# A hand-built schedule's activity sum for zero matmuls, and the table of thresholds that goes with it

## Chip, cores and metric

The kernel runs on one core of a Trainium2 chip. The metric is the device time of one execution in microseconds (us); times of the kernel before are the median of three runs. A core has five engines with their own instruction streams: TensorE (PE; its weight loads are listed as PEld), VectorE (DVE), ScalarE (ACT), GpSimd (POOL) and SyncE (SP, which issues the transfers). They meet through semaphores. TensorE's clock is granted by a throttle, and the profile lists the granted share.

## The reference

Four residual layers over 2048 tokens of width 512 with 32 heads of 16. Layers 0 and 2 are `_A_ref`: attention inside four segments of 512 tokens under the reference's mask, gated with a linear memory that is carried from segment to segment. Layers 1 and 3 are `_B_ref`: full attention over 2048 tokens. Cut to what matters:

```python
# A, for each segment s
logits = einsum('bhqd,bhkd->bhqk', qs, ks) * scale + mask
a_dot  = einsum('bhqk,bhkd->bhqd', softmax(logits), vs)
a_mem  = (phi(qs) @ M) / (phi(qs) @ z + 1e-6)
o      = g * a_mem + (1 - g) * a_dot
M, z   = M + phi(ks).T @ vs, z + phi(ks).sum()
# B
o = einsum('bhqk,bhkd->bhqd', softmax(q @ k.T * Dh ** -0.5), v)
# all
x = x + A(layernorm(x)); x = x + B(layernorm(x))   # twice, with the same weights
```

## The kernel before

The kernel is a Python program that writes out the instruction order of every engine in advance. `Sched.add` appends an instruction to its engine's list, works out what it must wait for, and calls `Sched.estimate`, which keeps a planned clock for each engine. The `Builder` reads these planned clocks whenever it decides what to put next, so one changed decision can shift everything after it.

The work comes in units. A unit takes two or three blocks of 128 keys by 512 queries of one head. TensorE computes the scores of a block with one matmul over 16 of the 32 rows that it addresses (four such row groups run side by side); the scores go into three PSUM banks; ScalarE takes the exponential of all of them in one instruction (line 1514), into `pT`. Units alternate between two sets of three banks, so TensorE fills one set while ScalarE empties the other. Later, TensorE multiplies the exponentials with the values. Where the output is token-major, these are matmuls with 34 or 51 streamed columns; in most of layers 1 and 3 (`fm`), the values are the 17 stationary columns (16 values and a column of ones for the denominator), 512 columns stream, and four such matmuls run side by side in four column groups of the array. They and the row-split score matmuls are what the weights of the activity sum distinguish, with tile shapes `rows < 128` and `cols < 128`.

ScalarE has more exponentials than it has time, so some blocks go to VectorE. `dx_first` (line 1121) writes a block's scores as 16-bit integers whose bits, read as bf16, approximate an exponential; `dx_shift` (line 1184) adds constants for further chords of the approximation, for one, two or four blocks at once. The tables call these decisions `DX_...`, `TAKEN`, `REST`, `QREST` and `PAIRS2`. Projections, layer norms, memory updates and output projections are background tasks, fitted between units by `background`, `bg_one` and `fits`, under credits `CR_...` and margins.

`keep_busy` is called at the end of each unit. It issues zero matmuls (a zero 128 by 128 weight against 512 columns of `wB`, which adds nothing to the result) while the activity of the last 3413 ns is below `FILL`, at most `FILLS` in a unit:

```python
        at = max(self.sc.t["act"] - 1330, min(soon, default=0.0) - self.HOR)
        while n < self.FILLS and self.sc.streamed(max(self.sc.t["pe"], at), 3413) < self.FILL:
            self.mm(self.ps[:, bank.col0:bank.col0 + 512], self.zero[:, :], self.wB[:, 0, 0:512], not own, not own,
```

`streamed` sums the weights that `estimate` has put into `self.streams` for each matmul. Before, a matmul counts its streaming time times 0.285 with fewer than 128 rows, times 0.38 with fewer than 128 columns, and in full otherwise.

`PIECES` is a table of 44 entries. When ScalarE's planned clock passes the first number (in us), the entry's values overwrite the builder's thresholds, so each 40 us stretch of the kernel has thresholds of its own.

Of the kernel before, what the change touches and what calls it, by code (L numbers as in the profile page):

```python
# [255 lines left out]


class Builder:
    NPU, NDX, FIT, MARGIN, PART, FILL_DVE, EARLY, FILL = 4, 5, 2, 450, 1, 300, 700, 0.5
# [11 lines left out]
    PIECES = [(20.0, {'DXA_REST': 14, 'EVAC_ACT': -300, 'LOW': 32}),  # L271
              (60.0, {'AHEAD': 500, 'CR_W': 1900, 'DXA_REST': 10, 'EVAC_ACT': -300, 'LOW': 24, 'wide': True}),
              (100.0, {'AHEAD': 500, 'CR_W': 1900, 'DQ': 1900, 'EVAC_ACT': -300, 'wide': True}),
              (140.0, {'AHEAD': 300, 'CR_W': 1400, 'DQ': 2200, 'DX_T': 480, 'EVAC_ACT': 0}),
              (180.0, {'DMA_LATE': 300, 'DX_FIN': 2500, 'DX_T': 480, 'PE_B': 5, 'PE_LOW': 5}),
              (220.0, {'DMA_LATE': 600, 'DX_FIN': 2000, 'DX_T': 430, 'LOW': 16, 'PE_B': 4, 'PE_LOW': 6, 'PVN': 6}),
              (260.0, {'DX_RES': 2, 'HOR': 100, 'LOW': 24, 'NEAR_N': 200, 'PVN': 4}),
              (300.0, {'DX_RES': 2, 'HOR': 100, 'MARGIN': 700, 'NEAR_N': 200}),
              (340.0, {'DMA_LATE': 300, 'DQ': 1900, 'DX_RES': 2, 'FILLS': 1, 'HOR': 100, 'MARGIN': 700, 'NEAR_E': 80, 'NEAR_N': 200}),
              (380.0, {'DMA_LATE': 300, 'DMA_STEPS': 3, 'DQ': 2500, 'DX_RES': 2, 'DX_T': 330, 'FILLS': 1, 'HOR': 100, 'MARGIN': 700, 'NEAR_E': 0, 'NEAR_N': 200}),  # L280
              (420.0, {'DMA_LATE': 300, 'DMA_STEPS': 3, 'DQ': 2500, 'DX_RES': 2, 'DX_T': 330, 'FILLS': 1, 'HOR': 100, 'MARGIN': 700, 'NEAR': 6, 'NEAR_E': 0, 'NEAR_N': 200}),
              (460.0, {'ALTA': (1, 9, 9, 9), 'DMA_LATE': 300, 'DMA_STEPS': 3, 'DQ': 2500, 'DX_RES': 2, 'DX_T': 330, 'FILLS': 1, 'HOR': 100, 'MARGIN': 700, 'NEAR': 10, 'NEAR_E': 0, 'NEAR_N': 200, 'TAKEN': 1.5}),
              (500.0, {'ALTA': (1, 1, 9, 9), 'CR_W': 1250, 'DMA_LATE': 600, 'DMA_STEPS': 2, 'DQ': 2200, 'DQN': 300, 'DX_RES': 0, 'DX_T': 430, 'FILLS': 2, 'HOR': 400, 'MARGIN': 450, 'NEAR_E': 60, 'NEAR_N': 130, 'TAKEN': 2.7}),
              (540.0, {'ALTA': (1, 1, 1, 1), 'CR_W': 1400, 'DQ': 2500, 'DQN': 600, 'PE_A': 4}),
              (580.0, {'DQ': 2200, 'FILLS': 1, 'FILL_DVE': 450, 'PART': 3, 'PE_A': 5}),
              (620.0, {'FILLS': 1, 'FILL_DVE': 450, 'NEAR_S': 30, 'PART': 3, 'SLACK': 150}),
              (660.0, {'FILLS': 2, 'FILL_DVE': 300, 'NEAR_S': 60, 'PART': 1, 'SLACK': 0}),
              (700.0, {'MARGIN': 700, 'SLACK': 0, 'TAKEN': 2.4}),
              (740.0, {'DQ': 2500, 'DX_LATE': 1500, 'MARGIN': 700, 'SLACK': 0, 'TAKEN': 2.4}),
              (780.0, {'DQ': 2200, 'DX_LATE': 3000, 'MARGIN': 450, 'PVHOLE': 250, 'PVLATE': 600, 'SLACK': 300, 'TAKEN': 2.7}),  # L290
              (820.0, {'BG_BANK': 0, 'PVHOLE': 100, 'PVLATE': 900, 'TAKEN': 3}),
              (860.0, {'AHEAD': 200, 'BG_BANK': 200, 'TAKEN': 2.7}),
              (900.0, {'AHEAD': 200, 'DX_LATE': 1500, 'DX_RES': 1}),
              (940.0, {'AHEAD': 200, 'DX_LATE': 1500, 'DX_RES': 1, 'FILL_DVE': 150, 'MARGIN': 700}),
              (980.0, {'AHEAD': 200, 'DX_LATE': 1500, 'DX_RES': 1, 'FILL_DVE': 150, 'MARGIN': 700, 'REST': 14}),
              (1020.0, {'AHEAD': 200, 'DVE_FIN': 1000, 'DX_LATE': 1500, 'DX_RES': 1, 'FILL_DVE': 150, 'MARGIN': 700, 'PART': 3, 'REST': 14}),
# [1 line left out]
              (1100.0, {'CARRY_W': 300, 'DMA_STEPS': 3, 'DXA_REST': 26, 'FILL': 0.35, 'LOW': 4, 'REST_N': 20}),
              (1140.0, {'CARRY_W': 0, 'DMA_STEPS': 2, 'DXA_REST': 10, 'FILL': 0.5, 'FILLS': 3, 'LOW': 4, 'PVN': 3, 'REST_N': 14}),
              (1180.0, {'FILLS': 3, 'LOW': 4, 'NEAR_S': 30, 'PVN': 2}),  # L300
              (1220.0, {'FILLS': 3, 'LOW': 4, 'MARGIN': 700, 'NEAR_S': 30, 'PVN': 2}),
              (1260.0, {'DVE_FIN': 1000, 'FILLS': 3, 'LOW': 4, 'MARGIN': 700, 'NEAR_S': 30, 'PVN': 2}),
              (1300.0, {'AHEAD': 200, 'BG_BANK': 400, 'DVE_FIN': 1000, 'DX_RES': 1, 'FILLS': 3, 'FILL_DVE': 150, 'LOW': 4, 'MARGIN': 700, 'NEAR_S': 30, 'PVN': 2}),
# [1 line left out]
              (1380.0, {'AHEAD': 200, 'BG_BANK': 400, 'DVE_FIN': 1000, 'DX_RES': 1, 'FILL': 0.45, 'FILLS': 3, 'FILL_DVE': 150, 'LOW': 4, 'MARGIN': 700, 'NEAR_S': 30, 'PVN': 2}),
              (1420.0, {'AHEAD': 200, 'BG_BANK': 400, 'DVE_FIN': 1000, 'DX_RES': 1, 'FILL': 0.45, 'FILLS': 3, 'FILL_DVE': 150, 'LOW': 4, 'MARGIN': 700, 'NEAR_S': 30, 'PVN': 2}),
              (1460.0, {'AHEAD': 200, 'BG_BANK': 400, 'DVE_FIN': 1000, 'DX_RES': 1, 'EVAC_ACT': -300, 'FILL': 0.45, 'FILLS': 2, 'FILL_DVE': 150, 'LOW': 4, 'MARGIN': 700, 'NEAR_S': 30, 'PVN': 2, 'REST': 14, 'REST_N': 20}),
              (1500.0, {'AHEAD': 200, 'BG_BANK': 400, 'DVE_FIN': 1000, 'DX_RES': 1, 'EVAC_ACT': -300, 'FILL': 0.45, 'FILL_DVE': 150, 'LOW': 4, 'MARGIN': 700, 'NEAR_S': 30, 'PVN': 2, 'REST': 14, 'REST_N': 20}),
              (1540.0, {'AHEAD': 200, 'BG_BANK': 400, 'DVE_FIN': 1000, 'DX_RES': 1, 'EVAC_ACT': -300, 'FILL': 0.45, 'FILL_DVE': 150, 'LOW': 4, 'MARGIN': 700, 'NEAR_S': 30, 'PVN': 2, 'REST': 11, 'REST_N': 20}),
              (1580.0, {'AHEAD': 200, 'BG_BANK': 400, 'DVE_FIN': 1000, 'DX_RES': 0, 'EVAC_ACT': -300, 'FILL': 0.45, 'FILL_DVE': 150, 'LOW': 4, 'MARGIN': 700, 'NEAR_S': 30, 'PVN': 2, 'REST': 5, 'REST_N': 20, 'TAKEN': 3.5}),  # L310
              (1620.0, {'AHEAD': 200, 'BG_BANK': 400, 'DVE_FIN': 1000, 'EVAC_ACT': -300, 'FILL': 0.45, 'FILL_DVE': 150, 'LOW': 4, 'MARGIN': 700, 'NEAR_S': 30, 'PVN': 2, 'REST': 5, 'REST_N': 20, 'TAKEN': 3.5}),
              (1660.0, {'AHEAD': 300, 'BG_BANK': 200, 'DVE_FIN': 600, 'DX_T': 530, 'EVAC_ACT': 0, 'FILL': 0.5, 'FILL_DVE': 300, 'LOW': 24, 'MARGIN': 450, 'NEAR_N': 200, 'NEAR_S': 60, 'PVN': 4, 'REST': 11, 'REST_N': 14, 'TAKEN': 3, 'TAKEN_N': 4}),
              (1700.0, {'DVE_FIN': 1000, 'DX_T': 530, 'NEAR_N': 200, 'TAKEN': 3, 'TAKEN_N': 4}),
              (1740.0, {'DVE_FIN': 1000, 'DX_T': 530, 'NEAR_N': 200, 'REST': 8, 'TAKEN': 3, 'TAKEN_N': 4})]
# [1571 lines left out]
```

## Time and profile before

| | us |
|---|---|
| median of three runs | 1774.92 |
| lowest, highest | 1773.96, 1778.8 |
| the profiled execution | 1777.42 |
| its span, first to last instruction | 1775.7 |
| mean granted TensorE clock in it | 0.989 |
| zero matmuls, TensorE busy with them | 175, 61.1 |

The page of the profile gives, in this order, the busy time of each engine, a picture of the span in 40 slices, the transfer queues, the chain of work that ended last and the costliest groups of instructions. In a row of a group stand the line, the engine, the operation, output and input, the shapes and the count; then busy time in us and mean ns of one; then the idle time of the engine just before, and what ended it. Matmuls have one line (445), since a helper issues them all, so they are told apart by their tiles. Four matmuls that run side by side show overlapping times; the engine's busy time counts each moment once. In the windows view, each row is a stretch of the span, with the busy time and (in brackets) the instructions of each engine, then the granted clock.

### The profile page before, as it was taken

The numbers are of one execution on the slowest core, as the hardware profiler recorded it, in microseconds if no ns is written. First come the engines' busy times: TensorE is split into PE (matmuls) and PEld (weight loads), VectorE is DVE, ScalarE is ACT, GpSimd is POOL, SyncE is SP. The second block draws the span as 40 slices with busy tenths as digits, with TensorE's granted clock in tenths as the row PEclk, the third lists the DMA queues.
The fourth block names the chain that finished last, engine by engine and source line by source line (L and its number), as shares of the span: only waits on it lengthen the run. The fifth ranks groups of instructions, "written<-read, shape, count | busy, mean of one in ns | idle before, by whom it ended". The sixth has DMA issues, their size and how long they took to land.

```text
span 1775.7 us, 42674 instructions
## 1 busy us (share of the span) xinstructions
PE 1586.7 (89%) x17429; PEld 564.7 (32%) x17429; DVE 1520.6 (86%) x3016; ACT 1733.2 (98%) x1680; POOL 287.4 (16%) x656
## 2 busy tenths in 40 slices
PE   8889899999998999999999989999888888888887
PEld 4445454452223222323222332332222222222222
DVE  6677867499985999798999789767999999999998
ACT  7999999999999999999999999999999999999998
POOL 4622415110005000203000330241100000000000
PEclk9999999999999999999999999999999999999999
DMA  6121111000101000000000010010000000000000
GB/s 173 22 47 32 29 17 26 14 12 4 16 7 16 1 13 13 8 13 19 1 13 13 16 23 13 16 22 13 2 13 1 1 1 13 1 1 7 7 1 13
DMA packets 86180, 30.01 MB, mean 17 GB/s; under 512 B 78816, under 2 KB 85472, under 8 KB 85984
## 3 DMA queue, kind: packets, MB, share of 16 engines
q1 hardware_dynamic: 85984, 27.29, 7.5%
...
q14 instruction: 60, 0.49, 0.1%
...
## 4 chain that ended last, share of the span: by engine, by line
ACT 50%; PE 22%; issue 16%; DVE 9%; POOL 2%; DMA 1%; SPq 0%; ACTq 0%; DVEq 0%; POOLq 0%
ACT pT L1514 49%; PE ps L445 22%; POOL pT L1529 2%; DVE KB L1121 1%; DVE VB L1121 1%; DVE dxw L1184 1%; ACT amem L697 0%; DVE dxw L1121 0%; DVE QA L1121 0%; DMA xT<-xn 0%; DVE KA L1121 0%; DVE KA L1646 0%; DVE KB L1184 0%; DVE x L911 0%; DVE VB L1184 0%
## 5 line engine op out<-in xcount | busy, mean ns | idle before, releaser
L1514 ACT ACTIVATE pT<-ps 128x1024 bf16<-128x1024 f32 (+4 forms) x1627 | 1700.1, 1193 | 27.9 <-PE ps L445 19.8
L445 PE MATMUL ps<-qm,KB 32*128 32x512 bf16 x3584 | 524.0, 386 | 97.8 <-ACT pT L1514 87.0
L445 PE MATMUL ps<-pT,VB 128*17 128x512 bf16 x2217 | 378.9, 387 | 10.5 <-ACT pT L1514 6.0
L1529 POOL TENSOR_SCALAR_AFFINE_SELECT pT<-pT 128x256 bf16<-128x256 bf16 (+2 forms) x524 | 211.8, 416 | 545.0 <-ACT pT L1514 533.0
L445 PEld LDWEIGHTS ps<-qm,KB 32*128 32x128 bf16 x3584 | 132.3, 91 | 465.7 <-ACT pT L1514 360.5
L1424 POOL TENSOR_SCALAR qm<-QB,par 128x512 bf16<-128x512 bf16 x88 | 68.2, 777 | 856.4 <-PE ps L445 782.8
L445 PEld LDWEIGHTS ps<-pT,VB 128*17 128x17 bf16 x2217 | 87.6, 87 | 244.2 <-issue 198.9
L1121 DVE TENSOR_SCALAR dxw<-ps 128x512 uint16<-128x512 f32 (+1 forms) x209 | 143.6, 698 | 5.3 <-PE ps L445 4.4
L445 PE MATMUL ps<-qm,QA 32*128 32x512 bf16 x512 | 111.4, 391 | 25.4 <-ACT pT L1514 22.7
L1184 DVE TENSOR_SCALAR dxw<-dxw 128x1024 uint16<-128x1024 uint16 (+1 forms) x315 | 125.2, 409 | 3.0 <-PE ps L445 1.3
L1121 DVE TENSOR_SCALAR QA<-ps 128x512 uint16<-128x512 f32 (+1 forms) x174 | 122.2, 715 | 5.4 <-PE ps L445 4.8
L445 PE MATMUL ps<-qm,KA 32*128 32x384 bf16 (+3 forms) x1024 | 103.4, 307 | 24.2 <-ACT pT L1514 20.0
L445 PE MATMUL ps<-VA,pT 128*128 128x51 bf16 (+1 forms) x2560 | 109.0, 189 | 14.0 <-POOL pT L1529 6.4
L1121 DVE TENSOR_SCALAR VA<-ps 128x512 uint16<-128x512 f32 (+1 forms) x159 | 114.0, 730 | 6.3 <-PE ps L445 5.5
L445 PE MATMUL ps<-dxw,VW 128*17 128x512 bf16 x435 | 110.6, 383 | 0.2 <-DVE dxw L1184 0.2
L445 PEld LDWEIGHTS ps<-VA,pT 128*128 128x128 bf16 x2560 | 86.2, 97 | 63.2 <-POOL pT L1529 29.7
L1121 DVE TENSOR_SCALAR KB<-ps 128x512 uint16<-128x512 f32 (+1 forms) x128 | 96.2, 769 | 2.8 <-PE ps L445 1.9
L445 PE MATMUL ps<-xT,wA 128*128 128x512 bf16 (+1 forms) x281 | 78.3, 381 | 1.5 <-DVE xT L658 0.9
L445 PE MATMUL ps<-pT,VA 128*17 128x512 bf16 x393 | 78.6, 387 | 1.2 <-ACT pT L1514 0.9
L1121 DVE TENSOR_SCALAR VB<-ps 128x512 uint16<-128x512 f32 (+1 forms) x99 | 74.7, 769 | 3.2 <-PE ps L445 2.6
L445 PE MATMUL ps<-dxw,VB 128*17 128x512 bf16 x256 | 74.3, 381 | 0.0
L445 PE MATMUL ps<-VB,pT 128*128 128x34 bf16 (+1 forms) x1788 | 69.5, 186 | 1.4 <-ACT pT L1514 1.1
...
## 6 DMA issues: line engine op xcount, KB each, us to landing
...
xT<-xn SPq DMA_TRANSPOSE x60, 2.4
oT<-ob SPq DMA_TRANSPOSE x36, 2.4
...
```

What stands on the lines that cost most here:

```text
L445: self.sc.add("pe", lambda e: e.matmul(out, lhsT, rhs, start=start, stop=stop, skip_group_check=True), reads=reads, banks=[(bank, "w", all ...
L1121: self.sc.add("dve", lambda e: e.tensor_scalar(d, o, SCALE * LOG2E * 128, W_C if dxs[0][:3] in self.wt else EXP_C, op0=ALU.mult, op1=ALU.add),
L1184: self.op("dve", lambda e: e.tensor_scalar(o, w, d, None, op0=ALU.add), reads=self.b_dxw[b0][:len(ents)], writes=wr, ns=(295, 425, 560, 69 ...
L1424: self.op(eng, (lambda m, q, col: lambda e: e.tensor_scalar(m, q, col, 0.0, op0=ALU.mult, op1=ALU.add))(m, q, col), reads=[bq, self.b_par] ...
L1514: self.sc.add("act", (lambda dst, src: lambda e: e.activation(dst, src, ACT.Exp, scale=SCALE))(dst, src), writes=self.b_pT[slot * 3 + i:sl ...
L1529: self.op("pool", (lambda blk, pat: lambda e: e.affine_select(blk, blk, pattern=pat, compare_op=ALU.is_ge, fill=0.0, base=0, channel_multi ...
```

## The change

The weights in `estimate` change. Row-split matmuls count 0.3 of their streaming time. Column-split matmuls count 0.85 of the time by which they extend the time already covered by such matmuls (`fm_end` holds its end). Of full matmuls, those with fewer than 100 streamed columns count 0.9. The default of `FILL` goes from 0.5 to 0.44. All 44 entries of `PIECES` are replaced by others with the same boundaries in time; a few are shown.

```diff
-        self.streams = []
+        self.streams, self.fm_end = [], 0.0
...
-            self.streams.append((st, n / 2.4 * (0.285 if rows < 128 else 0.38 if cols < 128 else 1)))
+            if rows < 128:
+                w = 0.3 * n / 2.4
+            elif cols < 128:
+                w = 0.85 * max(0.0, st + n / 2.4 - max(st, self.fm_end))
+                self.fm_end = max(self.fm_end, st + n / 2.4)
+            else:
+                w = n / 2.4 * (0.9 if n < 100 else 1)
+            self.streams.append((st, w))
...
-    NPU, NDX, FIT, MARGIN, PART, FILL_DVE, EARLY, FILL = 4, 5, 2, 450, 1, 300, 700, 0.5
+    NPU, NDX, FIT, MARGIN, PART, FILL_DVE, EARLY, FILL = 4, 5, 2, 450, 1, 300, 700, 0.44
...
-    PIECES = [(20.0, {'DXA_REST': 14, 'EVAC_ACT': -300, 'LOW': 32}),
-              (60.0, {'AHEAD': 500, 'CR_W': 1900, 'DXA_REST': 10, 'EVAC_ACT': -300, 'LOW': 24, 'wide': True}),
...
-              (1060.0, {'AHEAD': 300, 'CARRY_W': 300, 'DVE_FIN': 600, 'DX_LATE': 3000, 'DX_RES': 0, 'FILL': 0.35, 'FILL_DVE': 300, 'MARGIN': 450, 'PART': 1, 'REST': 11, 'REST_N': 20}),
...
-              (1340.0, {'AHEAD': 200, 'BG_BANK': 400, 'DVE_FIN': 1000, 'DX_RES': 1, 'FILL': 0.45, 'FILLS': 3, 'FILL_DVE': 150, 'LOW': 4, 'MARGIN': 700, 'NEAR_S': 30, 'PVN': 2}),
...
+    PIECES = [(20.0, {'CR_A': 1500, 'LOW': 32, 'PE_A': 3, 'TAKEN_N': 2}),
+              (60.0, {'CR_A': 1300, 'FILL': 0.5, 'LOW': 24, 'PE_A': 5, 'TAKEN_N': 3}),
+              (100.0, {'FILL': 0.5, 'FILLS': 1}),
+              (140.0, {'DXS': 2, 'DX_BANK': 300, 'FILL': 0.44, 'FILLS': 2, 'wide': True}),
...
+              (1340.0, {'DX_WAIT': 0, 'PAIRS2': 2, 'PVHOLE': 250, 'QREST': 30}),
...
```

The computation stays the same, with the same matmuls for scores and projections. Which blocks ScalarE takes and which VectorE, which wait for which, and the place of each background task follow from the new table.

More of the change, by code (lines that the diff above doesn't have):

```diff
@@ L270 @@
              [(-1.5, -6.7, -5.8, 20.8, 1.2), (-5.2, -1.6, 28.5, 28, 7), (21, 35.0, 8.2, 30, 27.7), (21, 48.0, 37, 23.6, 12.2)]]
-    PIECES = [(20.0, {'DXA_REST': 14, 'EVAC_ACT': -300, 'LOW': 32}),
-              (60.0, {'AHEAD': 500, 'CR_W': 1900, 'DXA_REST': 10, 'EVAC_ACT': -300, 'LOW': 24, 'wide': True}),
[L273 to L296, printed above, removed]
-              (1060.0, {'AHEAD': 300, 'CARRY_W': 300, 'DVE_FIN': 600, 'DX_LATE': 3000, 'DX_RES': 0, 'FILL': 0.35, 'FILL_DVE': 300, 'MARGIN': 450, 'PART': 1, 'REST': 11, 'REST_N': 20}),
[L298 to L303, printed above, removed]
-              (1340.0, {'AHEAD': 200, 'BG_BANK': 400, 'DVE_FIN': 1000, 'DX_RES': 1, 'FILL': 0.45, 'FILLS': 3, 'FILL_DVE': 150, 'LOW': 4, 'MARGIN': 700, 'NEAR_S': 30, 'PVN': 2}),
[L305 to L314, printed above, removed]
@@ new lines @@
+    PIECES = [(20.0, {'CR_A': 1500, 'LOW': 32, 'PE_A': 3, 'TAKEN_N': 2}),
+              (60.0, {'CR_A': 1300, 'FILL': 0.5, 'LOW': 24, 'PE_A': 5, 'TAKEN_N': 3}),
+              (100.0, {'FILL': 0.5, 'FILLS': 1}),
+              (140.0, {'DXS': 2, 'DX_BANK': 300, 'FILL': 0.44, 'FILLS': 2, 'wide': True}),
+              (180.0, {'CR_A': 1100, 'DXS': 1, 'DX_BANK': 500, 'PART': 4}),
+              (220.0, {'CR_A': 1300, 'MARGIN': 700, 'PART': 1, 'SLACK': 150}),
+              (260.0, {'BG_BANK': 100, 'LOW': 4, 'MARGIN': 700, 'SLACK': 150}),
+              (300.0, {'BG_BANK': 200, 'CR_B': 1700, 'DXS': 0, 'FILL_DVE': 150, 'LOW': 24, 'MARGIN': 700, 'SLACK': 300}),
+              (340.0, {'CR_B': 1500, 'DXS': 1, 'EARLY': 1000, 'FILL_DVE': 300, 'MARGIN': 450}),
+              (380.0, {'DX_RES': 3, 'EARLY': 1000, 'MARGIN': 700}),
+              (420.0, {'DX_RES': 3, 'EARLY': 1000, 'MARGIN': 700, 'PVN': 3}),
+              (460.0, {'DX_RES': 3, 'EARLY': 1000, 'MARGIN': 700, 'PVN': 3}),
+              (500.0, {'DX_RES': 3, 'EARLY': 700, 'MARGIN': 700, 'PVN': 3, 'REST': 8}),
+              (540.0, {'DVE_FIN': 300, 'DX_RES': 3, 'MARGIN': 700, 'PVN': 3, 'REST': 8, 'SLACK': 150}),
+              (580.0, {'DVE_FIN': 300, 'DX_RES': 3, 'DX_T': 480, 'FILL': 0.46, 'MARGIN': 700, 'PVN': 3, 'QREST': 16, 'REST': 8, 'SLACK': 300}),
+              (620.0, {'DVE_FIN': 600, 'DX_RES': 0, 'DX_T': 430, 'FILL': 0.44, 'FILLS': 1, 'MARGIN': 450, 'PVN': 4, 'QREST': 24, 'REST': 11}),
+              (660.0, {'CARRY_W': 300, 'FILLS': 1, 'QREST': 36}),
+              (700.0, {'CARRY_W': 300, 'CR_W': 1250, 'FILLS': 1, 'QREST': 36}),
+              (740.0, {'CARRY_W': 300, 'CR_W': 1250, 'FILLS': 1, 'QREST': 36}),
+              (780.0, {'CARRY_W': 300, 'CR_W': 1250, 'FILLS': 1, 'PVN': 6, 'QREST': 36, 'SLACK': 500}),
+              (820.0, {'CARRY_W': 0, 'CR_W': 1400, 'FILLS': 2, 'FILL_DVE': 150, 'PVN': 4, 'QREST': 24, 'SLACK': 500}),
+              (860.0, {'FILL_DVE': 150, 'NEAR_E': 40, 'PVN': 3, 'REST': 14, 'SLACK': 500}),
+              (900.0, {'AHEAD': 200, 'FILL_DVE': 300, 'NEAR_E': 60, 'PVN': 4, 'REST': 11, 'SLACK': 300}),
+              (940.0, {'AHEAD': 200, 'ALTA': (2, 9, 9, 9), 'FILL_DVE': 450}),
+              (980.0, {'AHEAD': 300, 'ALTA': (1, 1, 1, 1), 'DX_RES': 1, 'FILL_DVE': 300, 'LOW': 12, 'MARGIN': 700}),
+              (1020.0, {'DX_RES': 1, 'FILL_DVE': 450, 'FILL_FREE': 0.5, 'LOW': 12, 'MARGIN': 700}),
+              (1060.0, {'DMA_LATE': 0, 'DX_RES': 1, 'FILL_DVE': 450, 'FILL_FREE': 0.5, 'LOW': 12, 'MARGIN': 700}),
+              (1100.0, {'DMA_LATE': 0, 'DX_RES': 1, 'FILL_DVE': 450, 'FILL_FREE': 0.5, 'LOW': 4, 'MARGIN': 700}),
+              (1140.0, {'CR_LOW': 1300, 'DMA_LATE': 0, 'DX_RES': 1, 'EARLY': 1000, 'FILL_DVE': 450, 'FILL_FREE': 0.5, 'LOW': 4, 'MARGIN': 700, 'NEAR_S': 30}),
+              (1180.0, {'BG_BANK': 400, 'CR_LOW': 1300, 'DMA_LATE': 0, 'DX_RES': 1, 'EARLY': 1000, 'FILL_DVE': 450, 'FILL_FREE': 0.5, 'LOW': 4, 'MARGIN': 700, 'NEAR_S': 30, 'TAKEN_N': 2}),
+              (1220.0, {'BG_BANK': 400, 'CR_B': 1700, 'CR_LOW': 1300, 'DMA_LATE': 0, 'DX_LATE': 1500, 'DX_RES': 1, 'EARLY': 1000, 'FILL_DVE': 450, 'FILL_FREE': 0.5, 'LOW': 4, 'MARGIN': 700, 'NEAR_S': 30, 'REST': 17, 'TAKEN_N': 2}),
+              (1260.0, {'BG_BANK': 400, 'CR_B': 1700, 'CR_LOW': 1300, 'DMA_LATE': 0, 'DX_LATE': 1500, 'DX_RES': 1, 'EARLY': 1000, 'FILL_DVE': 450, 'FILL_FREE': 0.5, 'LOW': 4, 'MARGIN': 700, 'NEAR_S': 30, 'REST': 20, 'SLACK': 500, 'TAKEN_N': 2}),
+              (1300.0, {'BG_BANK': 200, 'CR_B': 1500, 'CR_LOW': 1900, 'DMA_LATE': 600, 'DX_LATE': 3000, 'DX_RES': 0, 'DX_WAIT': 0, 'EARLY': 700, 'FILL_DVE': 300, 'FILL_FREE': 1, 'LOW': 24, 'MARGIN': 450, 'NEAR_S': 60, 'REST': 11, 'SLACK': 300, 'TAKEN_N': 3}),
+              (1340.0, {'DX_WAIT': 0, 'PAIRS2': 2, 'PVHOLE': 250, 'QREST': 30}),
+              (1380.0, {'DX_WAIT': 0, 'PAIRS2': 2, 'PVHOLE': 250, 'QREST': 30}),
+              (1420.0, {'AHEAD': 200, 'DX_WAIT': 0, 'LOW': 4, 'PAIRS2': 2, 'PVHOLE': 250, 'PVN': 6, 'QREST': 30}),
+              (1460.0, {'AHEAD': 200, 'DX_T': 480, 'DX_WAIT': 0, 'FILL_DVE': 700, 'LOW': 4, 'PAIRS2': 2, 'PVHOLE': 250, 'PVN': 6, 'QREST': 30}),
+              (1500.0, {'AHEAD': 200, 'DX_T': 480, 'DX_WAIT': 0, 'FILL_DVE': 700, 'LOW': 4, 'NEAR': 14, 'NEAR_N': 200, 'NEAR_S': 0, 'PAIRS2': 2, 'PVHOLE': 250, 'PVN': 6, 'QREST': 30}),
+              (1540.0, {'AHEAD': 200, 'DVE_LATE': 700, 'DX_T': 480, 'DX_WAIT': 0, 'FILL_DVE': 700, 'LOW': 4, 'NEAR': 14, 'NEAR_N': 200, 'NEAR_S': 0, 'PAIRS2': 2, 'PVHOLE': 250, 'PVN': 6, 'QREST': 30}),
+              (1580.0, {'AHEAD': 300, 'DVE_LATE': 700, 'DX_LATE': 1500, 'DX_T': 480, 'DX_WAIT': 0, 'FILL_DVE': 700, 'GAP': 1, 'LOW': 4, 'NEAR': 14, 'NEAR_N': 200, 'NEAR_S': 0, 'PAIRS2': 2, 'PVHOLE': 250, 'PVN': 6, 'QREST': 30}),
+              (1620.0, {'DVE_LATE': 700, 'DX_LATE': 1500, 'DX_T': 480, 'DX_WAIT': 0, 'FILL_DVE': 700, 'GAP': 1, 'LOW': 4, 'NEAR': 14, 'NEAR_N': 200, 'NEAR_S': 0, 'PAIRS2': 2, 'PVHOLE': 250, 'PVN': 6, 'QREST': 30, 'REST': 14}),
+              (1660.0, {'DVE_LATE': 700, 'DX_LATE': 1500, 'DX_T': 480, 'DX_WAIT': 0, 'EARLY': 1000, 'FILL': 0.46, 'FILL_DVE': 700, 'GAP': 1, 'LOW': 4, 'NEAR': 14, 'NEAR_N': 200, 'NEAR_S': 0, 'PAIRS2': 2, 'PVHOLE': 250, 'PVN': 6, 'QREST': 30, 'REST': 14}),
+              (1700.0, {'DVE_LATE': 700, 'DX_LATE': 1500, 'DX_T': 480, 'DX_WAIT': 0, 'EARLY': 1000, 'FILL': 0.46, 'FILL_DVE': 700, 'GAP': 1, 'LOW': 4, 'NEAR': 14, 'NEAR_N': 200, 'NEAR_S': 0, 'PAIRS2': 2, 'PVHOLE': 250, 'PVN': 6, 'QREST': 30, 'REST': 14}),
+              (1740.0, {'DVE_LATE': 700, 'DX_LATE': 1500, 'DX_T': 480, 'DX_WAIT': 0, 'EARLY': 1000, 'FILL': 0.46, 'FILL_DVE': 700, 'GAP': 1, 'LOW': 4, 'NEAR': 14, 'NEAR_N': 200, 'NEAR_S': 0, 'PAIRS2': 2, 'PVHOLE': 250, 'PVN': 6, 'QREST': 30, 'REST': 5})]
```

## The prediction

> **What bounds the kernel now.** The page comes first: busy time by engine, the chain that ended last, and the costliest group.
>
> ```profile
> span 1775.7 us, 42674 instructions
> ...
> PE 1586.7 (89%) x17429; PEld 564.7 (32%) x17429; DVE 1520.6 (86%) x3016; ACT 1733.2 (98%) x1680; POOL 287.4 (16%) x656
> ...
> ACT 50%; PE 22%; issue 16%; DVE 9%; POOL 2%; DMA 1%; SPq 0%; ACTq 0%; DVEq 0%; POOLq 0%
> ...
> L1514 ACT ACTIVATE pT<-ps 128x1024 bf16<-128x1024 f32 (+4 forms) x1627 | 1700.1, 1193 | 27.9 <-PE ps L445 19.8
> ```
>
> ScalarE is busy 1733.2 of 1775.7 us, 1700.1 of them with the exponentials of line 1514. So the time is ScalarE's work plus the 42.5 us in which it stands. Other engines count only through these 42.5 us, or by taking exponentials off ScalarE. The windows view says where it stands (us, busy time and instructions of PE, PEld, DVE, ACT, POOL, then the granted clock, the DMA share and GB/s):
>
> ```profile
> core 0: us, PE busy (x) PEld busy (x) DVE busy (x) ACT busy (x) POOL busy (x), PEclk, DMA share, GB/s
> 0.00:40.00 40.00, 33.54 (x389) 18.45 (x389) 24.86 (x68) 30.60 (x42) 16.96 (x48) 1.00 0.67 189
> 42.00:47.00 5.00, 5.00 (x51) 2.33 (x51) 1.35 (x4) 4.18 (x5) 2.94 (x8) 0.66 0.00 0
> 83.00:88.00 5.00, 4.17 (x55) 2.81 (x55) 3.11 (x13) 3.74 (x6) 2.36 (x7) 0.66 0.26 52
> 274.00:279.00 5.00, 4.90 (x67) 2.79 (x65) 3.47 (x9) 4.15 (x6) 2.90 (x8) 0.66 0.42 28
> 557.00:562.00 5.00, 4.95 (x51) 2.11 (x52) 1.52 (x5) 4.38 (x5) 2.80 (x8) 0.66 0.07 14
> 1093.00:1102.00 9.00, 8.41 (x59) 1.50 (x58) 7.37 (x14) 7.67 (x8) 0.00 (x0) 0.62 0.06 13
> 1172.00:1181.00 9.00, 7.64 (x77) 3.96 (x77) 4.97 (x13) 6.55 (x6) 3.11 (x7) 0.62 0.22 44
> 1445.00:1450.00 5.00, 4.77 (x46) 0.96 (x43) 4.62 (x9) 4.21 (x5) 0.00 (x0) 0.66 0.01 3
> 1506.00:1511.00 5.00, 4.30 (x38) 0.84 (x38) 4.74 (x8) 4.51 (x5) 0.00 (x0) 0.66 0.01 3
> 1523.00:1528.00 5.00, 4.43 (x34) 0.98 (x34) 3.83 (x6) 4.10 (x5) 0.69 (x1) 0.66 0.01 3
> 1768.00:1776.00 8.00, 3.42 (x16) 0.93 (x14) 3.83 (x10) 1.56 (x3) 0.00 (x0) 1.00 0.20 66
> ```
>
> The start (40 − 30.60 = 9.4 us) and the end (7.7 of the span's last 1775.7 − 1768, less 1.56: 6.1) belong to filling and draining. Between them the clock falls nine times. In these nine stretches ScalarE stands 0.82 + 1.26 + 0.85 + 0.62 + 1.33 + 2.45 + 0.79 + 0.49 + 0.90 = **9.5 us**, about 1.06 for each. The other 17.5 us lie in small pieces. The waits of ScalarE agree:
>
> ```profile
> ACT pT L1514 <- PE ps L445: 19.8, 45, 2.1
> ACT x L954 <- PE ps L445: 3.5, 2, 2.7
> ACT pT L1514 <- POOL pT L1529: 2.8, 5, 0.8
> ```
>
> What comes ahead of a fall shows in windows of 3.41 us, the first three ending where the clock falls, the last an undisturbed one:
>
> ```profile
> 1442.11:1445.52 3.41, 2.25 (x22) 0.69 (x26) 3.38 (x5) 3.41 (x4) 0.00 (x0) 1.00 0.00 0
> 1503.55:1506.96 3.41, 2.35 (x19) 0.50 (x16) 3.38 (x6) 3.41 (x4) 0.66 (x1) 1.00 0.00 0
> 1520.62:1524.03 3.41, 2.17 (x27) 0.52 (x23) 3.34 (x6) 3.41 (x4) 0.00 (x0) 1.00 0.00 0
> 1600.00:1603.41 3.41, 2.82 (x31) 0.70 (x31) 3.25 (x5) 3.41 (x5) 0.00 (x0) 1.00 0.01 2
> ```
>
> So the clock falls after a thin window, not after an empty one: ScalarE was never late there, TensorE merely had less to stream. The zero matmuls exist to thicken such windows.
>
> **The change part by part.** Three things are edited: the weights in the builder's activity sum, the threshold against which it is held, and the table of 44 stretches. Since all queues follow from these, I counted instructions in the two programs.
>
> *Zero matmuls: 175 become 119.*
>
> ```profile
> L445 PE MATMUL ps<-wB,zero 128*128 128x512 bf16 x175 | 61.1, 394 | 0.0
> ```
>
> Each takes 61.1 / 175 = 0.35 us of TensorE; 56 fewer free 19.5 us. They are issued where the builder sees TensorE ahead of ScalarE, and ScalarE has only 19.8 − 8 = about 12 us of waits on TensorE outside the falls (most of the 9.5 us are such waits). I take 0; the bounds are 0 and −1 us (12 us by the zero matmuls' 61.1 of 1586.7 busy us would be 0.5). Where they went matters more. Cutting ScalarE's work into ten equal parts, the zero matmuls before are 15, 17, 17, 36, 20, 20, 23, 14, 4, 9, after 15, 6, 11, 21, 5, 15, 19, 10, 8, 9. The losses lie in parts 2 to 5; the last three parts hold 27 both times. A look at how matmuls run explains it:
>
> ```profile
> 1600.26 0.39 PE L445 MATMUL ps<-qm,KB 32*128 32x512 bf16 x4 [0.55 <-ACT pT L1514]
> 1600.81 0.38 PE L445 MATMUL ps<-KB,VW 128*17 128x512 bf16 x1
> ```
>
> Four K=32 matmuls start together; the old rule counted them as 4 × 0.285 = 1.14 of one, the new as 4 × 0.3 = 1.2. Four matmuls of 17 columns run together as well; the old rule counted 4 × 0.38 = 1.52, the new 0.85. So where 17-column matmuls prevail, as from 1220 us on, the new sum is much lower, and a threshold of 0.44 instead of 0.45 to 0.5 asks for more; in the first 400 us, which have none, sums hardly move and 0.44 asks for less. I summed both rules over matmul starts in the window ahead of each fall: the new one gives 0.24 to 0.37 at all nine, the old one 0.24 to 0.48. The new rule sorts the windows better.
>
> *ScalarE's work.* Exponentials of 1536, 1024, 768, 512 and 256 columns were 606, 862, 48, 55 and 56 and become 626, 829, 38, 98 and 44; ScalarE's evacuations in line 478 go from 13 to 12.
>
> ```profile
> L1514 ACT ACTIVATE pT<-ps 128x1536 bf16<-128x1536 f32 x606 | 872.1, 1501 | 16.3 <-PE ps L445 11.4 <-POOL pT L1529 1.8 <-POOL VB L882 0.9
> L1514 ACT ACTIVATE pT<-ps 128x1024 bf16<-128x1024 f32 x862 | 847.6, 1079 | 8.8 <-PE ps L445 6.4 <-POOL pT L1529 1.0 <-ACT pT L1514 0.2
> L1514 ACT ACTIVATE pT<-ps 128x768 bf16<-128x768 f32 x48 | 41.3, 861 | 1.2 <-PE ps L445 0.9
> L1514 ACT ACTIVATE pT<-ps 128x512 bf16<-128x512 f32 x55 | 31.0, 654 | 0.6 <-PE ps L445 0.5
> L1514 ACT ACTIVATE pT<-ps 128x256 bf16<-128x256 f32 x56 | 24.3, 434 | 0.9 <-PE ps L445 0.7
> L478 ACT ACTIVATE QB<-ps 128x512 bf16<-128x512 f32 x4 | 2.4, 603 | 0.0
> ```
>
> Successive exponentials overlap, so busy time by count is the price: 872.1/606 = 1.439, 847.6/862 = 0.983, 0.860, 0.564, 0.434 us. The sum is 20 × 1.439 − 33 × 0.983 − 10 × 0.860 + 43 × 0.564 − 12 × 0.434 = +6.8, less one evacuation of 0.6: **+6.2 us**. The column count agrees: 8192 more columns are 16 blocks of 512, each (1501 − 1079) ns = 0.42 more, 6.8. With single durations instead it would be 8.7 − 0.6 = 8.1, the upper end. These 16 blocks are the ones that VectorE no longer computes: 1039 before, 1023 after.
>
> *VectorE's side.*
>
> ```profile
> L1121 DVE TENSOR_SCALAR dxw<-ps 128x512 uint16<-128x512 f32 x203 | 136.3, 682 | 4.5 <-PE ps L445 3.7
> L1121 DVE TENSOR_SCALAR dxw<-ps x209: 656/682/1225, 113.1 to 1119.2; 128x512 uint16<-128x512 f32 x103, 128x1024 uint16<-128x1024 f32 x2
> L1184 DVE TENSOR_SCALAR dxw<-dxw 128x1024 uint16<-128x1024 uint16 x271 | 112.6, 425 | 2.4 <-PE ps L445 1.3
> L1184 DVE TENSOR_SCALAR VB<-KB 128x2048 uint16<-128x2048 uint16 x18 | 12.3, 686 | 0.2
> ```
>
> ```profile
> 1580.00:1760.00 180.00, 151.97 (x1523) 39.43 (x1519) 175.41 (x282) 180.00 (x168) 5.35 (x6) 1.00 0.01 4
> ```
>
> 54 fewer single first steps, 19 more double ones, 28 more two-block and 20 fewer four-block shifts: −54 × 0.682 + 19 × 1.225 + 28 × 0.425 − 20 × 0.686 = −15.4 us. It is hidden: in the 180 us of the second row VectorE is busy 175.41 and ScalarE never stands. What it costs is in ScalarE's term already. Transfers keep their count on SP's queue (167 entries in both); Pool has four entries fewer. Both cost nothing, since no wait of ScalarE of any size points at them.
>
> *The clock.* This is the one term that the rows bound only widely: from −9.5 us (no falls left) to +9.5 (twice as many). To choose, I laid the matmuls of each program beside their exponentials, with the durations above, and took the share of 3.41 us stretches in which the new rule's sum is below 0.44. In the last three parts it goes from 26% to 9%, in parts 2 to 7 from 6% to 11%; below 0.40 from 6% to 5% and from 1.8% to 4.7%. So the three late falls (2.2 us) become unlikely, and parts 2 to 7 get no safer. I take **−2.2 us**.
>
> The Trainium skill, "TensorE: Matmul & The Clock Gate" (Part 1), has the clock halved after at least one idle window of about 3.4 us, and advises only against gaps of that length. By that alone no zero matmul would matter here, and the falls would stay as they are; but TensorE was busy 2.17 to 2.35 of 3.41 us ahead of three falls, so the trace speaks against it.
>
> *Sum.* 1775.7 + 6.2 − 2.2 = 1779.7 us of span. The profiled execution took 1777.42 us, 1.7 around its span, and 2.5 more than the median of 1774.92; on the median's footing the result is 1774.92 + 4.0 = **1779 us**, 0.23% up. Under 0.3%, 5.3 us, I call it no change that a measurement can tell.
>
> **The rivals.**
> 1. *More falls* (slower). Parts 2 to 5 lose 47 of 90 zero matmuls, and thin stretches there become more frequent. If that brings five new falls at 1.06 us and none is saved, it is 6.2 + 5.3: 1786 us. It decides from the point where less than one fall is saved net (6.2 − 0.9 = 5.3). For it: the low stretches of parts 2 to 7. Against it: with 36 and 20 zero matmuls in parts 4 and 5 the old kernel had one fall there, so many were spare.
> 2. *Falls vanish* (faster by over 0.3%). It takes 11.5 us from the 42.5: all nine falls and 2 us of the 17.5 in small pieces, 1774.92 + 6.2 − 11.9 = 1769 us. For it: the new weights tell falls from other windows. Against: those at 43, 84 and 275 us sit in stretches with waits for transfers and Pool, which a table hardly plans for.
> 3. *The clock doesn't care.* Late counts are 27 and 27, and the nine falls stay: 1774.92 + 6.2 = 1781 us, 0.35% up. For it: the counts; against it: windows ahead of falls are thin.
>
> **How the numbers follow.** Forecast 0.53, rival 1 0.32, rival 2 0.09, rival 3 0.06. Faster is rival 2, 0.09; slower rivals 1 and 3, 0.38; the rest, 0.53, within 0.3%. The extremes are 1774.92 + 6.2 − 9.5 − 1 = 1770.6 and 1774.92 + 8.1 + 9.5 = 1792.5. All of the upper end needs both costs at their worst; I leave out what needs more than six new falls: 1771 to 1787.
>
> **What would show it.** Exponentials of line 1514: 1635 in number, about 1707 us busy, ScalarE in all about 1739. Zero matmuls: 119. Falls: six, none after 1400 us. ScalarE's idle time: about 40 us. I am wrong if busy time doesn't rise by about 6 us, or if falls number fewer than three or more than ten, or if a new wait on Pool or a transfer takes over 3 us from ScalarE.

## The result and the profile after

The changed kernel takes 1784.16 us (median of five, 1782.15 to 1786.14) against 1776.09 us (five runs, 1773.96 to 1779.74): 8 us more. The ratio on record is 1.0042 with a 95% interval of 1.0025 to 1.0059; it isn't the plain quotient of the medians, which is 1.0045. The time lies in the stated range; the ratio is above the 0.3% of the forecast's own case, though the interval reaches below it. The profiled execution took 1782.15 us with a span of 1780.4, and is the quickest of the five. Line numbers are seven higher than before.

The page of the changed kernel, with the busy time by engine, the chain and the costliest group:

```profile
span 1780.4 us, 42182 instructions
...
PE 1594.3 (90%) x17087; PEld 576.0 (32%) x17265; DVE 1506.6 (85%) x2981; ACT 1739.5 (98%) x1687; POOL 288.6 (16%) x652
...
ACT 51%; PE 24%; issue 16%; DVE 7%; POOL 1%; DMA 0%; SPq 0%; ACTq 0%; DVEq 0%; POOLq 0%
...
L1521 ACT ACTIVATE pT<-ps 128x1024 bf16<-128x1024 f32 (+4 forms) x1635 | 1707.0, 1202 | 23.0 <-PE ps L452 18.0
```

ScalarE's busy time rose from 1733.2 to 1739.5, by 6.3 us, and its idle time fell from 42.5 to 40.9. So in these two executions, the whole 4.7 us of span is more busy time of ScalarE, less a little waiting. By shape (ScalarE's groups of the changed kernel: busy us, mean ns, idle before):

```profile
L1521 ACT ACTIVATE pT<-ps 128x1536 bf16<-128x1536 f32 x626 | 900.5, 1507 | 12.0 <-PE ps L452 9.5 <-POOL pT L1536 0.8 <-POOL qm L1431 0.3
L1521 ACT ACTIVATE pT<-ps 128x1024 bf16<-128x1024 f32 x829 | 815.6, 1088 | 7.3 <-PE ps L452 5.4 <-POOL pT L1536 0.6 <-ACT pT L1521 0.2
L1521 ACT ACTIVATE pT<-ps 128x512 bf16<-128x512 f32 x98 | 55.7, 702 | 1.3 <-PE ps L452 1.2
```

Per instruction these are 1.439, 0.984 and 0.568 us, as before (1.439, 0.983, 0.564): nothing became slower, there is more of it.

The stretches with a lower clock, in the windows view of the changed kernel (columns as in the prediction):

```profile
85.00:90.00 5.00, 4.20 (x42) 2.06 (x43) 4.30 (x15) 3.57 (x5) 2.58 (x7) 0.66 0.46 81
204.00:213.00 9.00, 8.40 (x132) 5.59 (x128) 6.56 (x15) 6.40 (x6) 1.67 (x3) 0.62 0.38 46
269.00:278.00 9.00, 8.19 (x109) 4.32 (x108) 4.91 (x11) 7.25 (x12) 5.33 (x15) 0.62 0.22 46
784.00:793.00 9.00, 8.17 (x79) 2.88 (x76) 7.37 (x15) 7.04 (x7) 1.78 (x3) 0.62 0.23 46
```

A fall is a stretch at half clock; in these two traces it lasts one window of 3.41 us or two. There are four falls instead of nine, seven windows at half clock instead of eleven, and none from 800 us to the last units. But three of the four lie between 178 and 888 us, where the table dropped zero matmuls, and each of these lasts two windows. Before, the same part had two falls of one window each, and the two falls of two windows lay between 888 and 1220 us. In the four stretches ScalarE stands 1.43 + 2.60 + 1.75 + 1.96 = 7.7 us, against 9.5 us for nine before.

One execution is a poor count of falls, since it is the granted clock that differs between runs. Every run has its span and mean clock, so the windows at half clock can be counted as 2 × (1 − clock) × span / 3.413 us. (This includes the window or so at the very end.) Over the 30 runs of the kernel before that stand beside the first experiments it is 9.5 on average, over 24 later runs 10.2, over the five of the changed kernel **10.0**. So the averages show no window saved, and the profiled execution, with the fewest windows of the five, was a lucky one. The five runs spread from 7 to 14 windows, so that a difference of one or two either way isn't excluded. The kernel before shows what a window costs: a straight line through those 54 runs rises by 1.0 us of span for each window (correlation 0.92 and 0.97 in the two sets), from 1765 to 1766 us with none. The straight line shows that they go together; it isn't a separate proof that the windows cause all of it.

### The profile page after: what moved, and what is told of

Same layout as the page of the kernel before. It is cut to its first block, busy times and chain, and to the rows that moved or that the text cites. A ratio compares the mean times of both kernels' runs of the same rounds, so it can differ in the third digit from the quotient of the medians.

```text
span 1780.4 us, 42182 instructions
## 1 busy us (share of the span) xinstructions
PE 1594.3 (90%) x17087; PEld 576.0 (32%) x17265; DVE 1506.6 (85%) x2981; ACT 1739.5 (98%) x1687; POOL 288.6 (16%) x652
## 4 chain that ended last, share of the span: by engine, by line
ACT 51%; PE 24%; issue 16%; DVE 7%; POOL 1%; DMA 0%; SPq 0%; ACTq 0%; DVEq 0%; POOLq 0%
ACT pT L1521 50%; PE ps L452 23%; POOL pT L1536 1%; ACT amem L704 1%; DVE dxw L1128 1%; DVE QA L1128 1%; DVE xT L1128 0%; DVE KB L1128 0%; DVE x L918 0%; DVE dxw L1191 0%; DVE KA L1653 0%; DVE VA L1128 0%; DVE rg L816 0%; DVE VB L1128 0%; DVE KB L487 0%
## 5 line engine op out<-in xcount | busy, mean ns | idle before, releaser
L1521 ACT ACTIVATE pT<-ps 128x1024 bf16<-128x1024 f32 (+4 forms) x1635 | 1707.0, 1202 | 23.0 <-PE ps L452 18.0
L452 PE MATMUL ps<-qm,KB 32*128 32x512 bf16 x3584 | 514.1, 386 | 81.5 <-ACT pT L1521 65.2
L452 PE MATMUL ps<-pT,VB 128*17 128x512 bf16 x2231 | 385.2, 385 | 8.9 <-ACT pT L1521 3.8
L1128 DVE TENSOR_SCALAR dxw<-ps 128x512 uint16<-128x512 f32 (+1 forms) x199 | 135.9, 698 | 4.7 <-PE ps L452 4.0
L1191 DVE TENSOR_SCALAR dxw<-dxw 128x1024 uint16<-128x1024 uint16 (+1 forms) x294 | 118.4, 413 | 6.8 <-PE ps L452 5.0
L1128 DVE TENSOR_SCALAR VA<-ps 128x512 uint16<-128x512 f32 (+1 forms) x144 | 102.1, 723 | 5.6 <-PE ps L452 4.8
L1128 DVE TENSOR_SCALAR KB<-ps 128x512 uint16<-128x512 f32 (+1 forms) x115 | 89.1, 789 | 3.0 <-PE ps L452 2.5
L452 PE MATMUL ps<-dxw,VB 128*17 128x512 bf16 x279 | 81.0, 385 | 0.3 <-issue 0.3
L452 PE MATMUL ps<-VB,pT 128*128 128x51 bf16 (+1 forms) x1828 | 72.7, 187 | 3.2 <-ACT pT L1521 2.0
L452 PEld LDWEIGHTS ps<-VB,pT 128*128 128x128 bf16 x1828 | 60.1, 96 | 32.3 <-issue 16.4
```

The lines of the kernel that those rows point to most:

```text
L452: self.sc.add("pe", lambda e: e.matmul(out, lhsT, rhs, start=start, stop=stop, skip_group_check=True), reads=reads, banks=[(bank, "w", all ...
L1128: self.sc.add("dve", lambda e: e.tensor_scalar(d, o, SCALE * LOG2E * 128, W_C if dxs[0][:3] in self.wt else EXP_C, op0=ALU.mult, op1=ALU.add),
L1191: self.op("dve", lambda e: e.tensor_scalar(o, w, d, None, op0=ALU.add), reads=self.b_dxw[b0][:len(ents)], writes=wr, ns=(295, 425, 560, 69 ...
L1521: self.sc.add("act", (lambda dst, src: lambda e: e.activation(dst, src, ACT.Exp, scale=SCALE))(dst, src), writes=self.b_pT[slot * 3 + i:sl ...
```

## The experiments

Twelve kernels ran. Theories: A, the 8 us are ScalarE's 16 more blocks, and falls come on top alike in both kernels; B, zero matmuls stand in TensorE's way; C, the clock doesn't depend on them; D, the 8 us are mostly falls that moved; E and F, on rule and table apart; G and H, on where the falls lie; I, idle time absorbs more work for ScalarE.

### Zero matmuls taken out, the order left alone

After all engines' orders were fixed, the zero matmuls were struck from TensorE's list; what they had waited for is waited for by the next matmul.

```diff
     def finalize(self):
+        kept, last, swap, held = [], None, {}, []
+        for op in self.ops["pe"]:
+            if op.name == "fill":
+                swap[id(op)] = last
+                held += op.deps
+            else:
+                op.deps, held = op.deps + held, []
+                kept.append(op)
+                last = op
+        self.ops["pe"] = kept
...
```

The kernel before:

> The kernel before with its 175 zero matmuls taken out after the order of all engines was fixed, so that nothing else moves. Theory A: thin stretches become more frequent, at least 25 stretches of 3.41 us at half clock for its 11, and at 0.6 to 1 us each 10 to 25 us slower than before. Theory B: a few us faster, since TensorE is freed of 61 us. Theory C: 1774 to 1778 us, with about as many falls as before.

The changed kernel:

> The changed kernel with its 119 zero matmuls taken out in the same way. Theory A: 10 to 20 us slower than the changed kernel, 1794 to 1804 us. Theory C: 1782 to 1786 us.

Measured, one run each beside 1777.11 us for the kernel before: 1799.32 and 1796.55 us. Span and mean clock of the kernel before without zero matmuls, then of the changed one:

```profile
core 0: 1797.6 us, clock 0.955
```

```profile
core 0: 1794.8 us, clock 0.969
```

By mean clock, half-clock windows are 47 against 11 in the kernel before and 33 against 7 in the changed one; the spans are 21.9 and 14.4 us longer, 0.6 us for each window more. Theory C falls. For the kernel before without zero matmuls, the clock row of the page's 40 slices and a stretch that begins in its thirteenth slice; then the stretch of the same work with them:

```profile
PEclk9989999999995999989999989988999899999999
```

```profile
562.00:587.00 25.00, 22.76 (x252) 9.79 (x251) 14.48 (x28) 22.43 (x24) 10.87 (x27) 0.52 0.06 12
```

```profile
558.00:583.00 25.00, 22.90 (x260) 8.28 (x255) 20.59 (x41) 23.51 (x24) 7.49 (x18) 0.93 0.06 12
```

TensorE is busy 22.8 of 25 us, with the clock at half in nearly all of them: busy time alone didn't bring it back. Note also which of the two is quicker without zero matmuls: the changed one, by 2.8 us, although ScalarE has more to do. It has 14 or 15 windows fewer, at 0.6 us about 8.7 us, and less 6.3 for ScalarE's work that leaves 2.4. That its order leaves fewer thin stretches is how I read this; with one run each it is a hint.

### More zero matmuls, the order left alone

At the end of `keep_busy`, further zero matmuls are issued where the plan leaves TensorE idle before its next bank is free. The planned clocks are restored afterwards, so no other decision changes. `XFILL` is 0.5, 0.6 or 0.9, `XMAX` 2, 3 or 4; sums are by the new rule in both kernels.

```diff
+        while k < XMAX and sc.t["pe"] + 230 * (k + 1) < free:
+            seen = sum(w for t, w in self.xw + self.xs if t >= now - 3413) / 3413
+            if seen >= XFILL:
+                break
+            t, tiles, streams = dict(sc.t), list(sc.tiles), list(sc.streams)
+            op = sc.add("pe", ...)
+            sc.t, sc.tiles, sc.streams = t, tiles, streams
...
```

Before, 0.5:

> The kernel before, its order on every engine unchanged, with up to two more zero matmuls after a unit wherever the plan leaves TensorE idle before its next bank comes free and the new activity sum of the last 3.41 us is under 0.5 (57 more). Theory A (the 8 us between the kernels are ScalarE's 16 more blocks, 6.2 us, and falls of the clock come on top in both): falls become fewer, 3 to 7 us faster than before, 1769 to 1773 us. Theory B (zero matmuls stand in TensorE's way): 1776 us or more, with longer waits of ScalarE on TensorE. Theory C (the clock doesn't depend on them): 1775 to 1778, as many falls.

Changed, 0.5:

> The changed kernel with the same addition (59 more zero matmuls). Theory A: 3 to 6 us faster than the changed kernel, 1778 to 1781 us, and 6 to 8 us above the kernel before with the same addition. Theory D (the 8 us are mostly falls that moved to where zero matmuls were dropped): at most 3 us above the kernel before with its addition. Theory B: 1784 us or more.

Before, 0.6:

> The kernel before with up to three more zero matmuls after a unit while the sum is under 0.6 (280 more). Theory A: hardly a fall left, 1766 to 1771 us. Theory B: slower than with 57, since 223 more cost TensorE 0.2 us each where it may be late: 1774 us or more. Theory C: 1775 to 1778.

Changed, 0.6:

> The changed kernel with up to three more while the sum is under 0.6 (222 more). Theory A: hardly a fall left, 1773 to 1778 us, still 6 to 7 us above the kernel before with this addition. Theory D: no more than 3 us above it. Theory B: 1784 us or more.

Measured, with 30 runs of the kernel before at a median of 1777.23 us:

| version | us, median | ratio to before | 95% interval |
|---|---|---|---|
| before, 57 more | 1775.02 | 0.9994 | 0.9982 to 1.0005 |
| changed, 59 more | 1782.62 | 1.0036 | 1.0023 to 1.0049 |
| before, 280 more | 1773.23 | 0.9983 | 0.9973 to 0.9992 |
| changed, 222 more | 1780.56 | 1.0020 | 1.0009 to 1.0031 |

With 57 and 59 more, the ratios gain 0.06% (1.0042 to 1.0036 for the changed kernel), 1 us instead of theory A's 3 to 7 and 3 to 6, and for neither kernel is that clear of zero. With 280 and 222, the medians are 2 to 3 us above A's ranges, and there are three falls of one window in either profile. The busy times of ScalarE, before and changed, from the two pages:

```profile
PE 1600.7 (90%) x17461; PEld 582.5 (33%) x17709; DVE 1522.5 (86%) x3016; ACT 1732.8 (98%) x1680; POOL 287.9 (16%) x656
```

```profile
PE 1627.2 (91%) x17267; PEld 586.8 (33%) x17487; DVE 1507.7 (85%) x2981; ACT 1740.0 (98%) x1687; POOL 288.2 (16%) x652
```

With falls nearly gone from both, the medians are still 7.3 us apart (7.6 in the weaker pair), and the spans 1779.1 − 1771.3 = 7.8, of which ScalarE's busy time makes 1740.0 − 1732.8 = 7.2. That is theory A; D would have had 3 us at most. Busy time has some scatter of its own: the three profiles of the kernel before with none, 57 and 280 added have 1733.2, 1732.3 and 1732.8 us, and the five of the changed kernel with none, 59, 222, 85 and 114 added have 1739.0 to 1740.4. The kernel before with 280 more is quicker than both kernels of this case. In its windows view, the stretches of three late falls are whole again:

```profile
1445.00:1450.00 5.00, 5.00 (x51) 1.53 (x48) 5.00 (x9) 5.00 (x7) 0.00 (x0) 1.00 0.00 0
1506.00:1511.00 5.00, 4.38 (x45) 1.11 (x45) 4.74 (x8) 5.00 (x6) 0.00 (x0) 1.00 0.00 0
1523.00:1528.00 5.00, 4.10 (x47) 1.20 (x45) 4.93 (x9) 5.00 (x5) 0.00 (x0) 1.00 0.00 2
```

ScalarE is busy for all of the 15 us, where it stood 2.2 us of them.

A stronger dose:

> The kernel before with up to four more zero matmuls after a unit while the sum is under 0.9 (568 more, against 280 in the version with 0.6). If the three falls left there come from thin stretches that the plan shows: 1771 to 1773 us with one fall or none. If they come from stalls that the plan doesn't have: 1773 to 1774, with the same falls. Theory B (TensorE becomes late): 1775 us or more, and more idle time of ScalarE ended by TensorE.

It took 1783.65 us, a ratio of 1.0040 (1.0025 to 1.0056). Its page and the wait of ScalarE on TensorE:

```profile
PE 1659.8 (93%) x17731; PEld 600.8 (34%) x17997; DVE 1523.5 (85%) x3016; ACT 1737.1 (97%) x1680; POOL 289.0 (16%) x656
```

```profile
ACT pT L1555 <- PE ps L486: 22.9, 61, 1.4
```

With 280:

```profile
ACT pT L1555 <- PE ps L486: 17.2, 45, 1.8
```

Two windows at half clock are left, yet the span is 10.6 us longer than with 280. The exponentials wait 61 times for TensorE instead of 45, and 5.7 us longer. Another 4.3 us is ScalarE's busy time, 1737.1 against 1732.8, with the same instructions; single exponentials take no longer (1184 ns on average against 1190), so less of their time overlaps. Laid beside each other instruction by instruction, the difference grows in many small steps, about half of it before 1220 us. Theory B holds from some point between 280 and 568.

### Only where the new table has fewer, and only later

The same addition with 0.6 in the changed kernel, switched on by ScalarE's planned clock.

```diff
+        if not any(a * 1000 <= sc.t["act"] < b * 1000 for a, b in ((178, 888),)):
+            return
```

> The changed kernel with the zero matmuls of the 0.6 kind added only from 178 to 888 us (85 more), the parts where the new table has 47 fewer. Theory G (its falls lie where zero matmuls were dropped): most of the gain of adding them everywhere (1784.2 to 1780.6), so 1780 to 1782 us, with no more than one fall between 178 and 888. Theory H (falls lie anywhere): half or less of it, 1782.5 us or more.

With `((888, 1800),)` instead:

> The changed kernel with them added only after 888 us (114 more). Theory G: little gain, 1783 to 1785 us, with falls left between 178 and 888. Theory H: half or more of the gain, 1782.5 us or less.

The kernel before was at 1778.12 us here. From 178 to 888 us: 1782.29 us, a ratio of 1.0021 (1.0008 to 1.0035), like the 1.0020 with the addition everywhere and below the 1.0042 without, though the intervals overlap. The median lies just above theory G's range and below theory H's. That part of the profile in the changed kernel and in this version:

```profile
178.00:888.00 710.00, 640.58 (x7601) 254.41 (x7679) 588.34 (x1222) 697.33 (x695) 127.50 (x286) 0.99 0.07 13
```

```profile
178.00:888.00 710.00, 652.59 (x7715) 259.15 (x7809) 589.60 (x1224) 699.58 (x698) 129.82 (x293) 1.00 0.07 13
```

One fall is left between 178 and 888, at 271 us; elsewhere this profile has others, so that it counts seven windows like the changed kernel's. By the mean clocks, its twelve runs have 5.3 half-clock windows on average, against 10.0 without the addition and 3.0 with it everywhere. After 888 only: 1789.19 us, 1.0071 (1.0052 to 1.0090), with falls at 207, 272 and 787 us and 10.5 windows on average. So what there was to gain lay mostly in the parts that lost zero matmuls, as theory G has it. That the late addition makes the kernel slower than without was expected by neither theory. Beside the changed kernel, instruction by instruction, its profiled execution loses 3.8 us between 100 and 140 us, at falls in a part that is the same in both (the version from 178 to 888 has these falls too), and 3.9 us between 1040 and 1100, around a fall at 1043. The six runs, 1784.8 to 1792.8, are too alike for me to call it chance, and the number of windows doesn't explain it; the cause stays open.

### Sixteen more blocks of ScalarE's time

In the kernel before with 280 more zero matmuls, eight exponentials of 1024 columns are computed twice. The first copy writes what the second overwrites.

```diff
+        for n in range(1600, 0, -200):
+            i = next(i for i in range(n, len(acts)) if acts[i].name == "exp1024")
+            op = Op("act", -1, acts[i].fn, "again")
+            op.deps = list(acts[i].deps)
+            op.emit = True
+            acts[i].deps.append(op)
+            acts.insert(i, op)
```

> The kernel before with 280 more zero matmuls, and with 8 exponentials of 1024 columns computed twice (each into the same place, ahead of the one that counts, which waits for it): 16 blocks more for ScalarE, with all else in place. Theory A (16 blocks more cost their own duration, since ScalarE has no slack): 8 times 0.9 to 1.2 us more than without them, 1773.2 + 7.2 to 9.6 = 1780.4 to 1782.8 us. Theory I (idle time takes up part of it, and the 7.3 us between the two kernels come largely from elsewhere): less than 4 us more, under 1777.2.

It took 1783.65 us, 1.0035 (1.0021 to 1.0048). The median is 0.9 us above theory A's range; but the kernel before was slower in these runs too, and by the ratios (1.0035 and 0.9983) it is 0.0052 of 1778, 9.2 us, above the version without, inside theory A's 7.2 to 9.6. Its runs also have 1.4 half-clock windows more on average. The page:

```profile
PE 1604.5 (90%) x17461; PEld 582.5 (33%) x17709; DVE 1523.4 (85%) x3016; ACT 1741.2 (98%) x1688; POOL 288.8 (16%) x656
```

ScalarE's busy time is 8.4 us more than without. Theory I falls: idle time took up none of this work.

### Rule and table apart

The new weights and threshold with the old table, without the table's own entries for `FILL`:

```diff
-            self.streams.append((st, n / 2.4 * (0.285 if rows < 128 else 0.38 if cols < 128 else 1)))
+            if rows < 128:
+                w = 0.3 * n / 2.4
+            elif cols < 128:
+                w = 0.85 * max(0.0, st + n / 2.4 - max(st, self.fm_end))
...
-    NPU, NDX, FIT, MARGIN, PART, FILL_DVE, EARLY, FILL = 4, 5, 2, 450, 1, 300, 700, 0.5
+    NPU, NDX, FIT, MARGIN, PART, FILL_DVE, EARLY, FILL = 4, 5, 2, 450, 1, 300, 700, 0.44
...
-              (1100.0, {'CARRY_W': 300, 'DMA_STEPS': 3, 'DXA_REST': 26, 'FILL': 0.35, 'LOW': 4, 'REST_N': 20}),
+              (1100.0, {'CARRY_W': 300, 'DMA_STEPS': 3, 'DXA_REST': 26, 'LOW': 4, 'REST_N': 20}),
...
```

> The new weights and the threshold 0.44 with the old table (its own thresholds for zero matmuls left out). It has 1016 blocks on VectorE and 167 zero matmuls. Theory E (rule and table each cost little by themselves; the time goes with the blocks left to ScalarE): 23 blocks more on ScalarE than before at 0.42 us, 1786 us. Theory F (the table only fits the order that it was made on, and another rule shifts every later decision): ScalarE is left waiting, over 1795 us with more than 55 us of ScalarE's idle time.

The new table with the old weights:

> The new table with the old weights. It has 1000 blocks on VectorE and 186 zero matmuls. Theory E: 39 blocks at 0.42 us, 1792 us. Theory F: over 1800 us with more than 55 us of ScalarE's idle time.

They took 1822.84 and 1824.35 us. The pages, rule alone and table alone:

```profile
span 1821.1 us, 42271 instructions
...
PE 1579.8 (87%) x17143; PEld 570.0 (31%) x17322; DVE 1507.7 (83%) x3000; ACT 1751.0 (96%) x1683; POOL 291.0 (16%) x664
```

```profile
span 1822.6 us, 42131 instructions
...
PE 1616.2 (89%) x17091; PEld 589.2 (32%) x17282; DVE 1496.8 (82%) x2956; ACT 1755.7 (96%) x1679; POOL 286.4 (16%) x660
```

Both halves are worse than either whole, by 39 to 47 us, in one run each: ScalarE is busy 18 and 22 us more than before (1733.2), of which 23 and 39 more blocks at 0.42 us make 10 and 16, and it stands 70 and 67 us. By their mean clocks (0.982 and 0.974) the runs have 19 and 28 half-clock windows. That is theory F as far as the time goes. Its reason is argued and not shown: the entries of a table answer to one order, and with a few zero matmuls more or fewer early on, the later entries meet other units than they were chosen for. The new rule and the new table together are only 8 us from the old pair.

## Why the prediction was right or wrong

*What bounds the kernel.* Right: the doubled exponentials cost their time in full, and adding 280 zero matmuls to TensorE cost nothing.

*ScalarE's work.* Forecast 6.2 us, measured 6.3 in the profiled pair and 7.2 in the pair with few falls. The exponentials were to be about 1707 us busy and are 1707.0. Pricing by busy time over count, in which overlapping instructions count once, was better than single durations (8.1).

*Zero matmuls at nothing, VectorE hidden.* The changed kernel has 119, as counted. ScalarE's waits of line 1521 on TensorE went from 19.8 to 18.0 us; VectorE lost 14.0 us against the 15.4 worked out, and nothing came of it. The cover isn't endless: 568 more zero matmuls used it up.

*The clock.* In the profiled pair this term came out nearly as taken: ScalarE stands 7.7 us in the falls instead of 9.5, 1.8 us less where −2.2 was forecast. There are four falls where six were expected, with none after 1400 us, and parts 2 to 7 have six half-clock windows both times. The pair's spans differ by 4.7 us, against the 4.0 worked out. That so much fits is in part luck, since it is one execution of each, and the one of the changed kernel the quickest of five. The averages over the runs (9.5 and 10.2 half-clock windows before, 10.0 after, where the five runs leave an uncertainty of about 1) show no gain, so the −2.2 us are not borne out there. Where the falls lie in the other runs is not on record. What the step left out is what fewer zero matmuls in parts 2 to 5 would cost: adding some between 178 and 888 us brought the average from 10.0 to 5.3 windows. My own figures pointed there (stretches under 0.44 going from 6% to 11%), and rival 1 said how, but I gave them no price in the sum. Rival 1 was too dear at five falls net: on average, as many windows came as went.

*The sum.* 6.3 us by ScalarE and nothing by the clock is 1782.4 us from the median of 1776.09; the measured 1784.16 leaves 1.8 us. The pair with few falls is 7.3 us apart, so up to 1 us more may be ScalarE's time. The median of five runs before is also a low one: from 1777.23 and 1778.12, its medians over 30 and 24 later runs, to 1784.16 it is 6.9 and 6.0 us. The rest is within the interval (1.0025 to 1.0059 is 4.4 to 10.5 us). The rise of 8.1 us, or 0.42% by the ratio, is nearest rival 3's 6.2 us and 0.35%, while the time itself is nearer rival 1's 1786 us. But rival 3's reason is wrong: falls do depend on zero matmuls, and only their number came out about equal.

*When the clock falls.* The windows of 3.41 us ahead of the three falls between 178 and 888 us in the changed kernel, each ending where the clock falls:

```profile
201.49:204.90 3.41, 2.48 (x50) 1.48 (x50) 3.34 (x6) 3.41 (x4) 2.74 (x7) 1.00 0.00 0
266.39:269.80 3.41, 2.76 (x53) 1.67 (x50) 3.17 (x9) 3.41 (x5) 2.77 (x6) 1.00 0.02 5
781.80:785.21 3.41, 2.63 (x45) 1.45 (x41) 3.34 (x6) 3.41 (x4) 2.28 (x6) 1.00 0.00 0
```

TensorE was busy 2.48 to 2.76 us in them, more than ahead of the prediction's three falls (2.17 to 2.35) and close to its undisturbed window (2.82). So busy time alone doesn't tell which window brings a fall; whether the new rule's sum does was not worked out for these three.

The Trainium skill, "TensorE: Matmul & The Clock Gate" (Part 1), halves the clock after an idle window of about 3.4 us and gives it back after a busy one. The runs disagree on both: falls came after windows with TensorE busy over 2 of 3.41 us, and without zero matmuls the clock stayed at half for 7 windows on end, in a stretch with TensorE busy 22.8 of 25 us. Its window of 3413 ns agrees: with zero matmuls, falls last 3.4 or 6.8 us.
